# Attention, router and two expert layers on one core: gate steps spread over two head pairs, gathers and weight parts reordered at the stage change

## The chip, the cores and the metric

One NeuronCore of a Trainium2 chip runs the whole program in one launch. The metric is device time in microseconds (us), the median of several runs; lower is better. The engines are called PE (TensorE, the matrix engine), DVE (VectorE), ACT (ScalarE), POOL (GpSimd) and SP (SyncE, which here only issues DMAs).

## The reference

Three layers follow each other. First attention with pooled queries (4 batches, 8 heads, 1152 keys, head size 64; two neighbouring queries are averaged, so 576 queries a head). Its output, 2304 tokens by 512, goes through a top-1 mixture of 8 experts, and then through a bilinear layer.

```
q_pool = q.reshape(B, H, S // 2, 2, D).mean(axis=3)
attn = softmax(q_pool @ k^T / sqrt(D)) ; x = (attn @ v) as [2304, 512]
logits = x @ w_gate ; e = argmax(logits) ; g = softmax(logits)[e]
x = g * (relu(x @ w1[e]) @ w2[e])          # 8 experts, 512 -> 1024 -> 512
out = ((x @ w_a) * (x @ w_b)) @ w_out      # 512 -> 1536 -> 512
```

## The kernel before, in words

**Number format.** Every f32 operand is split into a high and a low f16 part, and a product is three f16 matmuls. The subtraction that makes a low part ("split_low", `p_low`) is elementwise work for DVE or POOL.

**Attention** runs 16 head pairs (`NPAIR`), each in 21 units (`NU`), in one loop over `n` whose code order is the order on every engine (`manual_schedule`). A pair does two things at once. It computes scores, exponentials and the product with V of pair p (lines 365 to 430). And it finds the row maxima of pair p+1: `a_units` (line 315) makes a [128, 2, 384] block of scores on PE in the PSUM pool `ps_a`, which has two buffers (tag "sa"), and DVE reduces it (line 335, 14 such reductions in a pair). `finish_max` (line 341) turns the maxima into a column of the operand, by way of the small tile `mm` (line 345). POOL makes the low parts `pl` (line 406), one per unit.

**The same two "sa" buffers** also serve the transposes `tp` of `turn` (line 486), the logits `lp` and the gate's counts `rp`. While `tp` waits for `turn_low`, the reductions have one buffer left.

**The gate** of a finished batch (four pairs) is a generator: `scales`, `gate` and `out_scale` (lines 526, 543, 605) `yield` between steps, and the attention loop calls `aside()` as often in unit u as the table `ASIDE` (line 935) says. It is started in unit 15 of pairs 4, 8 and 12. It finds the expert of each token, counts ranks with six small matmuls into `rp` (line 564), and builds for each of 5 token tiles a one-hot table `amat` [128, 128] (line 593). The gate of the last batch cannot lie beside attention: it runs at the end.

**The stage change.** After the last pair: `norm`, `mag_x`, `turn`, `scales`, `logits`, `gate`, then `route` (line 641), which computes the row numbers of the first three token groups (`find(0)`, index tile `idx0`) and the slot table `info`. Then `gather` (line 1100, an indirect DMA on POOL) reads 128 tokens from the DRAM buffer `xbuf` into a tile `xg`; `scale_x` and `x_t` (lines 1110, 1117) scale and transpose them. Ten `warm` matmuls (line 1272) stand on PE between `info` and the transposes. A conditional (line 1281) reloads the weights if expert 0 has no token; PE's first matmul of the first slot waits until ACT and DVE have passed it. Before it the code puts four `split_low` of weight parts 12 to 15 on DVE, and four `load_raw(0, i, 2)` on SP.

**The experts** run in slots of 64 tokens (`do_slot`, line 1291): `stage1`, `stage2`, `change` (which splits the next expert's weights, 24 parts at an expert's end) and `finish`. After slot 0 `find(1)` computes the other index rows on DVE and PE. From slot 24 on, three `conv_step` a slot prepare weights of the last layer (lines 774 to 792, mostly DVE).

**The last layer** (lines 1350 to 1440) is a loop of matmuls on 384 tokens a step.

Of the kernel before, what the change touches and what calls it, by code (L numbers as in the profile page):

```python
# [27 lines left out]
def attn_moe_kernel(  # L28
# [114 lines left out]
    nc.vector.tensor_scalar(out=out_id, in0=iota_part, scalar1=float(PAD), scalar2=None, op0=ALU.add)  # L143

# [22 lines left out]
    offs = rt.tile([128, E], F32, name="offs")  # L167
    idxo = rt.tile([128, NT // 128], U32, name="idxo")
# [171 lines left out]
    def finish_max(p, halves=(0, 1)):  # L340
# [4 lines left out]
        nc.vector.tensor_scalar(  # L345
            out=mm, in0=mm, scalar1=-1.0 / MC, scalar2=float(np.log(PX)) * 16.0 * SC * SC / MC, op0=ALU.mult, op1=ALU.add
        )
# [103 lines left out]
    def norm(p, j):  # L451
        b, h = bh(p)
        if h == 0 and j == 0:
            xe[b] = ap2.tile([128, NTB, XW], F32, tag="xe", name=f"xe{b}")
            lgp[b] = ap2.tile([128, NTB, HP, E], F32, tag="lgp", name=f"lgp{b}")
# [43 lines left out]
    def logits(p):  # L499
# [3 lines left out]
        for t in range(NTB):  # L503
# [6 lines left out]
        nc.vector.tensor_scalar(  # L510
            out=lgp[b][:, :, h // 2], in0=lp[:, 0 : NTB * E].rearrange("p (t e) -> p t e", e=E),
            scalar1=1.0 / (VC * VC), scalar2=None, op0=ALU.mult,
        )
# [29 lines left out]
    def gate(b):  # L543
        lg = ap2.tile([128, NTB, E], F32, tag="lg", name=f"lg{b}")
        nc.vector.tensor_reduce(out=lg, in_=lgp[b].rearrange("p t h e -> p t e h"), axis=AX.X, op=ALU.add)
# [25 lines left out]
        yield  # L571
# [20 lines left out]
        for i in range(NTB):  # L592
            (nc.gpsimd if b == B - 1 and i < 3 else nc.vector).tensor_scalar(
                out=amat[:, b, i], in0=iota_row2.rearrange("p a r -> p (a r)"), scalar1=row[:, i], scalar2=None, op0=ALU.is_equal
            )
            if i == 2:
                yield
# [16 lines left out]


    def find(i, ip):
        NB = B * NTB
        c0, n = ((0, NP0), (NP0, NP - NP0))[i]
        bm = rt.tile([128, NB, 2, n], F16, name=f"bm{i}")
        w = [128, NB, 2, n]  # L620
        nc.vector.tensor_tensor(
            out=bm, in0=slot.rearrange("p t (o a) -> p t o a", o=1).to_broadcast(w),
            in1=iota_slot[:, :, c0 : c0 + n].rearrange("p (o a) s -> p o a s", o=1).to_broadcast(w), op=ALU.is_equal,
# [231 lines left out]
    with tc.manual_schedule():  # L855
# [195 lines left out]
        for i in range(8, 12):  # L1051
            split_pool(0, i)
# [4 lines left out]
        while gates:  # L1057
            aside()
# [207 lines left out]
    with tc.manual_schedule():  # L1266
# [24 lines left out]
        def do_slot(s):  # L1291
# [15 lines left out]
            if s == 0:  # L1307
                find(1, ipb)
# [141 lines left out]
```

## Time and profile before

| | us |
|---|---|
| median of 3 runs | 1330.67 (1327.02 to 1331.19) |
| the profiled execution, its own time | 1324.79 |
| its span in the trace | 1323.1 |

| stage | stretch of the span, us |
|---|---|
| attention | 0 to 558 |
| last gate, routing, first gather | 558 to 589 |
| experts | 589 to 883 |
| last layer | 887 to 1323 |

| engine | busy, share of the span |
|---|---|
| PE | 1189.3 us, 90% |
| DVE | 788.9 us, 60% |
| ACT | 648.6 us, 49% |
| POOL | 524.8 us, 40% |

An engine is busy while an instruction of it is in flight, also when that instruction itself is held up. So two columns are read together below: the duration of an instruction against the same form elsewhere, and the idle time before it, in square brackets with the instruction that ended it. "Granted clock" is the TensorE clock in a stretch, 1.00 being 2.4 GHz and 0.50 being 1.2 GHz. Times are positions in the span.

### The profile page before, as it was taken

The numbers are of one execution on the slowest core, as the hardware profiler recorded it, in microseconds if no ns is written. First come the engines' busy times: TensorE is split into PE (matmuls) and PEld (weight loads), VectorE is DVE, ScalarE is ACT, GpSimd is POOL, SyncE is SP. The second block draws the span as 40 slices with busy tenths as digits, with TensorE's granted clock in tenths as the row PEclk, the third lists the DMA queues.
The fourth block names the chain that finished last, engine by engine and source line by source line (L and its number), as shares of the span: only waits on it lengthen the run. The fifth ranks groups of instructions, "written<-read, shape, count | busy, mean of one in ns | idle before, by whom it ended". The sixth has DMA issues, their size and how long they took to land. (4 is left out here: it accounts for less than half of the span.)

```text
span 1323.1 us, 41118 instructions
## 1 busy us (share of the span) xinstructions
PE 1189.3 (90%) x17154; PEld 827.8 (63%) x17154; DVE 788.9 (60%) x1548; ACT 648.6 (49%) x1324; POOL 524.8 (40%) x475
## 2 busy tenths in 40 slices
PE   7799997999899889748987997889999999999996
PEld 6466664665566556547977997875555555555553
DVE  4677777878777876756377248528668732222221
ACT  3577885888688768804266237315433311111111
POOL 3578885888688868742243321200000000000000
PEclk9899998999899989858988998999999999999998
DMA  7656685456465622634077226503212100000000
GB/s 170 112 129 163 141 178 138 112 114 150 101 109 132 138 58 51 216 98 155 23 273 274 71 62 199 177 13 112 96 65 96 48 1 1 24 24 25 25 17 32
DMA packets 170508, 136.46 MB, mean 103 GB/s; under 512 B 101072, under 2 KB 136400, under 8 KB 170256
## 3 DMA queue, kind: packets, MB, share of 16 engines
q1 hardware_dynamic: 167056, 122.74, 35.2%
q0 software_dynamic: 3200, 10.53, 2.4%
q8 instruction: 136, 2.23, 0.7%
q14 instruction: 116, 0.95, 0.2%
HBM read 94.96 MB, written 9.74 MB: 79 GB/s over the span
## 5 line engine op out<-in xcount | busy, mean ns | idle before, releaser
L406 POOL TENSOR_TENSOR pl<-pt,ph 128x512 f16<-128x512 f32 (+1 forms) x330 | 382.4, 1176 | 130.5 <-ACT ph L388 97.9
L335 DVE TENSOR_REDUCE mx<-sa 128x2 f32<-128x768 f32 x224 | 206.4, 924 | 87.9 <-PE sa L330 85.0
L386 ACT ACTIVATE pt<-sp 128x512 f32<-128x512 f32 (+1 forms) x336 | 197.3, 588 | 116.6 <-PE sp L379 111.5
L1360 PEld LDWEIGHTS <-wc 128*128 128x128 f16 x1728 | 169.5, 98 | 124.5 <-PEq L1322 4.4
L1360 PE MATMUL ab<-x2h,wc 128*128 128x384 f16 x1152 | 212.0, 327 | 4.3 <-PEq L1322 4.3
L428 PEld LDWEIGHTS <-ph 128*128 128x128 f16 (+1 forms) x2880 | 152.9, 102 | 77.1 <-issue 37.2
L388 ACT ACTIVATE ph<-sp 128x512 f16<-128x512 f32 (+1 forms) x331 | 194.6, 588 | 0.0
L1399 POOL DMA_INDIRECT out_dram<-ob,idxo x18 | 17.7, 982 | 442.2 <-DVE ob L1398 409.8
L330 PE MATMUL sa<-kst,qq 128*128 128x384 f16 x480 | 162.2, 338 | 29.2 <-DVE mx L335 25.8
L428 PE MATMUL av<-vv,ph 128*128 128x65 f16 (+2 forms) x2880 | 170.3, 197 | 0.0
L330 PE MATMUL sa<-kst,qlt 128*128 128x384 f16 x480 | 161.4, 337 | 0.0
L428 PE MATMUL av<-vv,pl 128*128 128x65 f16 (+1 forms) x1440 | 157.9, 196 | 1.3 <-POOL pl L406 1.3
L1370 DVE TENSOR_TENSOR gf<-ab,sa 128x384 f32<-128x384 f32 x72 | 40.1, 557 | 192.5 <-PE ab L1360 192.5
L379 PE MATMUL sp<-rl,k2b 66*128 66x512 f16 (+1 forms) x576 | 138.9, 295 | 9.4 <-DMA rl<-qln 8.8
L376 PE MATMUL sp<-qq,kst 128*128 128x512 f16 (+1 forms) x576 | 138.2, 294 | 8.3 <-ACT ph L388 8.2
L1161 PEld LDWEIGHTS <-w2c 128*128 128x128 f16 x3840 | 127.2, 101 | 25.5 <-issue 18.3
L1140 PE MATMUL hp<-xh,w1c 128*128 128x64 f16 x2560 | 126.9, 195 | 8.1 <-DVEq L1281 2.5
L1140 PEld LDWEIGHTS <-w1c 128*128 128x128 f16 x3840 | 122.2, 100 | 14.0 <-DVE w1c L847 5.4
L428 PEld LDWEIGHTS <-pl 128*128 128x128 f16 (+1 forms) x1440 | 124.9, 103 | 1.6 <-POOL pl L406 1.6
L1140 PE MATMUL hp<-xl,w1c 128*128 128x64 f16 x1280 | 123.4, 195 | 1.6 <-issue 1.6
L1360 PE MATMUL ab<-x2l,wc 128*128 128x384 f16 x576 | 117.5, 327 | 0.0
L1161 PE MATMUL yp<-hh,w2c 128*128 128x64 f16 x2560 | 111.3, 198 | 5.6 <-ACT hh L1146 4.7
(229 smaller groups left out, 1813.5 us busy)
## 6 DMA issues: line engine op xcount, KB each, us to landing
raw<-in_moe_w_dram SPq DMA_DIRECT2D x20, 1024.0 KB, 6.5
rbw<-in_moe_w_dram SPq DMA_DIRECT2D x20, 1024.0 KB, 6.9
kr<-in_k_dram SPq DMA_DIRECT2D x16, 576.0 KB, 5.1
vr<-in_v_dram SPq DMA_DIRECT2D x16, 576.0 KB, 5.8
qr<-in_q_dram SPq DMA_DIRECT2D x32, 256.0 KB, 3.4
cl<-in_moe_w_a_dram SPq DMA_DIRECT2D x12, 512.0 KB, 3.5
cl<-in_moe_w_b_dram SPq DMA_DIRECT2D x12, 512.0 KB, 3.5
cl<-in_moe_w_out_dram SPq DMA_DIRECT2D x12, 512.0 KB, 3.6
```

Of the source, the lines that this page charges most:

```text
L330: nc.tensor.matmul(sa[:, i, :KA], lhsT=x[:, 128 * b_ : 128 * b_ + 128], rhs=kst[:, j, ks], start=o == 0, stop=o == len(ops) - 1,)
L335: nc.vector.tensor_reduce(out=s["mx"].rearrange("p t n -> p (t n)")[:, ones[0] : ones[0] + m].rearrange("p (m o) -> p m o", o=1), in_=sa[: ...
L376: nc.tensor.matmul(sp[:, o : o + w], lhsT=s["kst"][:, j, ks], rhs=s["qq"][:, c0 : c0 + w], start=True, stop=False)
L379: nc.tensor.matmul(sp[:, o : o + w], lhsT=k2b[p % 3][:, j, ks], rhs=s["rl", j if w > 64 else 1][0:66, c0 : c0 + w], start=False, stop=True,)
L386: nc.scalar.activation(pt[:, :o], sp[:, :o], AF.Exp, scale=1.0 / (16.0 * SC * SC))
L388: nc.scalar.activation(phb[n % NPB][0][:, :o], sp[:, :o], AF.Exp, scale=1.0 / (16.0 * SC * SC))
L406: eng.tensor_tensor(out=l[:, :w], in0=pts.pop(n)[:, :w], in1=h[:, :w], op=ALU.subtract)
L428: nc.tensor.matmul(o, lhsT=a, rhs=b_, start=first, stop=False, skip_group_check=True)
L1140: nc.tensor.matmul(hp[:, j], lhsT=wc[:, t, i], rhs=g[x][:, i, w], start=first, stop=(j == 3 and i == KD - 1 and x == "xl"), skip_group_che ...
L1161: nc.tensor.matmul(y[:, d], lhsT=wc[:, t, 128 * d : 128 * d + 128], rhs=hs[s, n][x][:, j], start=first, stop=(n == 1 and len(terms) == 1 a ...
L1360: nc.tensor.matmul(ps[:, 0:TB], lhsT=w_[:, t, m, 128 * i : 128 * i + 128], rhs=x_[:, i, ts_], start=(i + j == 0), stop=(j == 2 and i == KD ...
L1370: nc.vector.tensor_tensor(out=gf, in0=pair[1], in1=sa, op=ALU.mult)
```

## The change

The parts, in the order of the program:

- `mm` and the one-hot tables `amat` on DVE: an instruction with two tensor inputs in place of one with one tensor input.
- `lgp` sums the four logits products as they come, and the later reduction (`lg`) falls away.
- The gate's steps get more `yield`s, and `ASIDE` one call in every second unit; each of the five `amat` has a step of its own. `norm_tail` moves from unit 5 to 6.
- Two of the four parts that POOL split at the end of attention go to DVE.
- `xgb`, the gathers' targets, move from the pool `mp`, which shares memory with attention's tiles, to `rt`, which doesn't. The first `scale_x` goes to ACT.
- The conditional stands ahead of the four `split_low` and the four `load_raw`.
- `find(1)` is cut in two: its DVE part after slot 0, its matmuls after slot 1.
- `conv_step`s start at slot 17.

```
+    lpx = cst.tile([128, 9, 1], F32, name="lpx")          # memset to the added constant
+    xgb = [rt.tile([128, XW], F32, name=f"xg{i}") for i in range(3)]     # was mp.tile
 finish_max:
-        nc.vector.tensor_scalar(out=mm, in0=mm, scalar1=-1.0 / MC, scalar2=..., op0=ALU.mult, op1=ALU.add)
+        nc.vector.scalar_tensor_tensor(out=mm, in0=mm, scalar=-1.0 / MC, in1=lpx, op0=ALU.mult, op1=ALU.add)
 logits:
+        if h == 0:
+            nc.vector.tensor_scalar(out=lgp[b], in0=l_, scalar1=1.0 / (VC * VC), scalar2=None, op0=ALU.mult)
+        else:
+            nc.vector.scalar_tensor_tensor(out=lgp[b], in0=l_, scalar=1.0 / (VC * VC), in1=lgp[b], op0=ALU.mult, op1=ALU.add)
 gate:
-        lg = ap2.tile([128, NTB, E], F32, tag="lg", name=f"lg{b}")
-        nc.vector.tensor_reduce(out=lg, in_=lgp[b].rearrange("p t h e -> p t e h"), axis=AX.X, op=ALU.add)
+        lg = lgp[b]
...
         nc.vector.tensor_reduce(out=fm, in_=o, axis=AX.X, op=ALU.max)
+        yield
         nc.vector.tensor_tensor(out=o, in0=desc_, in1=fm.to_broadcast([128, NTB, E]), op=ALU.is_equal)
+        yield
+
+        yield
         yield
...
-        yield                                              # between the rp matmuls and the ranks
...
         for i in range(NTB):
-            (nc.gpsimd if b == B - 1 and i < 3 else nc.vector).tensor_scalar(
-                out=amat[:, b, i], in0=iota_row2..., scalar1=row[:, i], scalar2=None, op0=ALU.is_equal
-            )
-            if i == 2:
-                yield
+            if b == B - 1 and i < 3:
+                nc.gpsimd.tensor_scalar(out=amat[:, b, i], in0=io, scalar1=row[:, i], scalar2=None, op0=ALU.is_equal)
+            else:
+                nc.vector.tensor_tensor(out=amat[:, b, i], in0=io, in1=row[:, i].to_broadcast([128, 128]), op=ALU.is_equal)
+            yield
 attention loop:
-        ASIDE = [1, 0, 1, 0, 0, 1, 0, 1, 0, 0, 1, 0, 1, 0, 0, 1, 1, 0, 1, 1, 2]
+        ASIDE = [1, 0] * (NU // 2) + [1]
-            n0=13, n1=4, nt=5, ...
+            n0=13, n1=4, nt=6, ...
 end of attention:
-        for i in range(8, 12):
+        for i in range(10, 12):
             split_pool(0, i)
...
+        split_low(0, 8)
         turn_low(NPAIR - 1)
+        split_low(0, 9)
         logits(NPAIR - 1)
 scale_x:
-        (nc.gpsimd if pr else nc.vector).tensor_scalar(out=g["xs"]..., scalar1=g["x"][:, DM : DM + 1], ...)
+        if pr:
+            nc.gpsimd.tensor_scalar(...)
+        else:
+            nc.scalar.activation(xs_, g["x"][:, 0:DM], AF.Copy, scale=g["x"][:, DM : DM + 1])
 before slot 0:
         x_t(0)
-        for i in range(12, 16):
-            split_low(0, i)
-        for i in range(4):
-            load_raw(0, i, 2)
         e0 = field("n0", 0, wengs, E - 1)
         with tc.If(e0 > 0):
...
+        for i in range(12, 16):
+            split_low(0, i)
+        for i in range(4):
+            load_raw(0, i, 2)
 do_slot:
             if s == 0:
-                find(1, ipb)
+                find(1, ipb, (0,))                         # the two DVE instructions that make bm
+            if s == 1:
+                find(1, ipb, (1,))                         # 20 matmuls and the index conversion
             if 2 <= s < NU64 - 1:
...
-                for _ in range(3 if s >= 24 else 0):
+                for _ in range(3 if s >= 17 else 0):
```

Three places show the moves. Rows of before carry line numbers of the kernel before; rows of the change carry its own, which are 3 to 24 higher.

DVE in the pair after a gate has started, before (`mx` the maxima, `sa_14` and `sa_16` the score blocks, `xtl` the end of `norm_tail`):

```order
L475 RECIPROCAL rec<-rec 64x1
L477 TENSOR_SCALAR xtl<-av_9_3277,rec 64x64
L593 TENSOR_SCALAR amat<-iota_row_106,row_3603 128x128 x3
L335 TENSOR_REDUCE mx_3379<-sa_14_3738 128x2
L593 TENSOR_SCALAR amat<-iota_row_106,row_3603 128x128 x2
L598 TENSOR_TENSOR val<-tok_base,row_3603 128x5
L335 TENSOR_REDUCE mx_3379<-sa_16_3774 128x2
```

DVE at the same place with the change (`rp` the counts, `rank` the ranks), and then a later stretch in the pair after that:

```order
L478 TENSOR_SCALAR xtl<-av_9_3282,rec 64x64
L338 TENSOR_REDUCE mx_3380<-sa_14_3720 128x2
L338 TENSOR_REDUCE mx_3380<-sa_16_3753 128x2
L580 TENSOR_REDUCE tot_3773<-rp_3765 128x8
L581 TENSOR_TENSOR rank_3772<-rp_3765,run 128x40
```

```order
L603 TENSOR_TENSOR amat<-iota_row_106,row_3890 128x128
L338 TENSOR_REDUCE mx_4035<-sa_0_4036 128x2
L603 TENSOR_TENSOR amat<-iota_row_106,row_3890 128x128
L338 TENSOR_REDUCE mx_4035<-sa_2_4101 128x2
L258 SCALAR_TENSOR_TENSOR vv_215<-vr_3553,vv_215 128x9x64
L338 TENSOR_REDUCE mx_4035<-sa_4_4137 128x2
L603 TENSOR_TENSOR amat<-iota_row_106,row_3890 128x128 x2
L338 TENSOR_REDUCE mx_4035<-sa_6_4185 128x2
```

The three `amat` in a row ahead of `sa_14` are gone from there; `tot` and `rank`, which stood behind `sa_4` of the same run of blocks, come behind `sa_16`, and the five `amat` are spread over the stretch in which the next pair begins.

DVE between attention and the first slot, before (`osc` the last attention result, `xl` the low part of the first tokens, `w2c` the weight parts; the last two rows are the conditional):

```order
L612 SCALAR_TENSOR_TENSOR osc<-gs_10594 128x5
L1112 TENSOR_SCALAR xs_10630<-xg_10627 128x512
L1124 SCALAR_TENSOR_TENSOR xl_10633<-xt_10646,xh_10632 128x512
L847 SCALAR_TENSOR_TENSOR w2c_9831<-raw_154,w2c_9831 128x512
L847 SCALAR_TENSOR_TENSOR w2c_9832<-raw_154,w2c_9832 128x512
L847 SCALAR_TENSOR_TENSOR w2c_9833<-raw_154,w2c_9833 128x512
L847 SCALAR_TENSOR_TENSOR w2c_9834<-raw_154,w2c_9834 128x512
L1168 TENSOR_LOAD info
L1281 COMPARE_AND_BRANCH
```

The same place with the change:

```order
L620 TENSOR_TENSOR gs_10589<-gs_10589,am_10441 128x5
L621 SCALAR_TENSOR_TENSOR osc<-gs_10589 128x5
L1145 SCALAR_TENSOR_TENSOR xl_10625<-xt_10638,xh_10624 128x512
L1189 TENSOR_LOAD info
L1298 COMPARE_AND_BRANCH
```

`xs` has gone to ACT, and the four `w2c` come after the conditional.

DVE after slot 0, before (`x2l` the slot's result, `bm`, `idf`, `idx` the rest of the indices, `hl` of the next slot):

```order
L1178 SCALAR_TENSOR_TENSOR x2l<-yp_10650,x2h 128x4x64
L621 TENSOR_TENSOR bm_11198<-slot,iota_slot 128x760
L625 TENSOR_TENSOR bm_11198<-bm_11198,val 128x760
L636 TENSOR_SCALAR idf_11221<-ipb,pad_id 64x19 x2
L639 CAST idx_142<-idf_11221 128x19
L1147 SCALAR_TENSOR_TENSOR hl_0_10641<-hp_10648,hh_0_10640 128x256
```

With the change:

```order
L1199 SCALAR_TENSOR_TENSOR x2l<-yp_10642,x2h 128x4x64
L652 TENSOR_TENSOR bm_11190<-slot,iota_slot 128x760
L656 TENSOR_TENSOR bm_11190<-bm_11190,val 128x760
L1168 SCALAR_TENSOR_TENSOR hl_0_10633<-hp_10640,hh_0_10632 128x256
L1168 SCALAR_TENSOR_TENSOR hl_1_10635<-hp_10641,hh_1_10634 128x256
```

`idf` and `idx` follow one slot later, and with them the 20 matmuls on PE from which they come.

## Rows read from the trace of the kernel before

**Rows 1.** Head pairs: stretch, length; busy PE, PEld, DVE, ACT, POOL; clock, DMA, GB/s

```profile
294.26:323.58 29.32, 28.30 (x428) 18.93 (x425) 23.29 (x41) 24.84 (x52) 26.09 (x25) 1.00 0.65 156
193.98:234.84 40.86, 32.36 (x435) 20.94 (x432) 33.60 (x71) 25.33 (x53) 25.20 (x23) 0.87 0.49 123
...
453.92:494.20 40.28, 32.37 (x434) 20.90 (x431) 32.97 (x70) 25.33 (x53) 25.21 (x23) 0.87 0.31 68
```

**Rows 2.** PE timeline, plain pair, then gate pair: start, us, instruction, [idle before]

```profile
181.59 0.32 PE L330 MATMUL sa<-kst,qq 128*128 128x384 f16 x1 [0.81 <-DVE mx L335]
...
199.14 0.32 PE L330 MATMUL sa<-kst,qq 128*128 128x384 f16 x1 [1.31 <-DVE mx L335]
...
202.96 0.19 PE L564 MATMUL rp<-oh,ones 128*128 128x40 f16 x1 [2.58 <-DVE oh L558]
...
219.72 0.48 PE L330 MATMUL sa<-kst,qq 128*128 128x384 f16 x1 [4.00 <-DVE mx L335]
```

**Rows 3.** DVE timeline around the first gate

```profile
164.00 1.00 DVE L345 TENSOR_SCALAR mm<-mm 128x9 f32<-128x9 f32 x1
...
199.01 0.42 DVE L545 TENSOR_REDUCE lg<-lgp 128x40 f32<-128x160 f32 x1
...
201.80 1.10 DVE L558 TENSOR_TENSOR oh<-desc,gfm 128x40 f16<-128x40 f32 x1
...
215.51 3.16 DVE L593 TENSOR_SCALAR amat<-iota_row,row 128x128 f16<-128x128 f32 x3
...
219.58 0.47 DVE L593 TENSOR_SCALAR amat<-iota_row,row 128x128 f16<-128x128 f32 x2
```

**Rows 4.** POOL timeline of the same stretch

```profile
163.82 1.16 POOL L406 TENSOR_TENSOR pl<-pt,ph 128x512 f16<-128x512 f32 x1 [0.25 <-ACT ph L388]
...
201.70 1.15 POOL L406 TENSOR_TENSOR pl<-pt,ph 128x512 f16<-128x512 f32 x1 [2.22 <-issue]
...
214.10 4.49 POOL L406 TENSOR_TENSOR pl<-pt,ph 128x512 f16<-128x512 f32 x4
```

**Rows 5.** PE timeline from the end of attention to the second slot

```profile
542.30 0.47 PE L489 MATMUL tp<-ident,xe 128*128 128x128 f32 x1 [1.88 <-DMA xe<-xtl]
...
577.45 4.61 PE L1272 MATMUL yp<-ones_sq 128*128 128x128 f32 x20 [0.73 <-DVE gs L607]
583.74 1.09 PE L1121 MATMUL xt<-ident,xs 128*128 128x128 f32 x4 [1.69 <-issue]
...
588.83 0.23 PE L1140 MATMUL hp<-xh,w1c 128*128 128x64 f16 x1 [2.51 <-DVEq L1281]
...
599.27 0.66 PE L629 MATMUL ipb<-bm,amat 128*128 128x38 f16 x20 [2.77 <-DVE bm L625]
```

**Rows 6.** The other engines' timelines of that stretch, by start

```profile
572.44 0.17 DVE L639 CAST idx<-idf 128x3 uint32<-128x3 f32 x1
...
578.07 0.17 DVE L612 SCALAR_TENSOR_TENSOR osc<-gs 128x5 f32<-128x5 f32 x1
...
579.28 1.20 POOL L1102 DMA_INDIRECT xg<-xbuf,idx  x1 [8.81 <-issue]
...
583.15 0.49 DVE L1112 TENSOR_SCALAR xs<-xg 128x512 f32<-128x512 f32 x1 [4.92 <-DMA xg<-xbuf,idx]
...
585.62 0.69 DVE L1124 SCALAR_TENSOR_TENSOR xl<-xt,xh 128x512 f16<-128x512 f32 x1 [1.98 <-ACT xh L1123]
586.23 2.49 DVE L847 SCALAR_TENSOR_TENSOR w2c<-raw,w2c 128x512 f16<-128x512 f32 x4
```

**Rows 7.** Stages after the wait at 599.27, columns as in rows 1

```profile
600.00:602.00 2.00, 2.00 (x43) 2.00 (x40) 0.62 (x3) 0.00 (x0) 1.01 (x1) 0.50 0.00 0
602.00:604.00 2.00, 2.00 (x52) 2.00 (x50) 0.42 (x1) 0.38 (x1) 0.00 (x0) 0.66 0.52 140
```

**Rows 8.** Stages, three slots with two expert changes: without and with conversions

```profile
690.10:718.11 28.01, 22.55 (x592) 21.37 (x592) 24.53 (x43) 20.93 (x43) 8.11 (x5) 0.88 0.85 302
800.73:833.43 32.70, 23.36 (x590) 22.18 (x587) 30.51 (x56) 23.64 (x49) 6.50 (x4) 0.84 0.78 267
```

More of the change, by code (lines that the diff above doesn't have):

```diff
@@ L454, in norm @@
             xe[b] = ap2.tile([128, NTB, XW], F32, tag="xe", name=f"xe{b}")
-            lgp[b] = ap2.tile([128, NTB, HP, E], F32, tag="lgp", name=f"lgp{b}")
+            lgp[b] = ap2.tile([128, NTB, E], F32, tag="lgp", name=f"lgp{b}")
             nc.gpsimd.memset(xe[b][64:128, 4], 0.0)
@@ L509, in logits @@
                 )
[L510 to L513, printed above, removed]
+        l_ = lp[:, 0 : NTB * E].rearrange("p (t e) -> p t e", e=E)
+        if h == 0:
+            nc.vector.tensor_scalar(out=lgp[b], in0=l_, scalar1=1.0 / (VC * VC), scalar2=None, op0=ALU.mult)
+        else:
+            nc.vector.scalar_tensor_tensor(
+                out=lgp[b], in0=l_, scalar=1.0 / (VC * VC), in1=lgp[b], op0=ALU.mult, op1=ALU.add
+            )
     def store_x(b, h0, h1):
@@ L592, in gate @@
         for i in range(NTB):
[L593 to L597 removed]
+            io = iota_row2.rearrange("p a r -> p (a r)")
+            if b == B - 1 and i < 3:
+                nc.gpsimd.tensor_scalar(out=amat[:, b, i], in0=io, scalar1=row[:, i], scalar2=None, op0=ALU.is_equal)
+            else:
+                nc.vector.tensor_tensor(
+                    out=amat[:, b, i], in0=io, in1=row[:, i].to_broadcast([128, 128]), op=ALU.is_equal
+                )
+            yield
         nc.vector.tensor_tensor(
@@ L613, in out_scale, with find @@
         yield
-    def find(i, ip):
+    bms = {}
+    def find(i, ip, halves=(0, 1)):
         NB = B * NTB
         c0, n = ((0, NP0), (NP0, NP - NP0))[i]
-        bm = rt.tile([128, NB, 2, n], F16, name=f"bm{i}")
+        if 0 in halves:
+            bms[i] = rt.tile([128, NB, 2, n], F16, name=f"bm{i}")
+        bm = bms[i]
         w = [128, NB, 2, n]
-        nc.vector.tensor_tensor(
-            out=bm, in0=slot.rearrange("p t (o a) -> p t o a", o=1).to_broadcast(w),
-            in1=iota_slot[:, :, c0 : c0 + n].rearrange("p (o a) s -> p o a s", o=1).to_broadcast(w), op=ALU.is_equal,
-        )
-        nc.vector.tensor_tensor(
-            out=bm, in0=bm, in1=val.rearrange("p b i (o a) -> p (b i) o a", o=1).to_broadcast(w), op=ALU.mult
-        )
+        if 0 in halves:
+            find_places(bm, w, c0, n)
+        if 1 not in halves:
+            return
         for t in range(NB):
@@ L639, in find, with find_places @@
         nc.vector.tensor_copy(idxs[i], idf)
+    def find_places(bm, w, c0, n):
+        nc.vector.tensor_tensor(
+            out=bm, in0=slot.rearrange("p t (o a) -> p t o a", o=1).to_broadcast(w),
+            in1=iota_slot[:, :, c0 : c0 + n].rearrange("p (o a) s -> p o a s", o=1).to_broadcast(w), op=ALU.is_equal,
+        )
+        nc.vector.tensor_tensor(
+            out=bm, in0=bm, in1=val.rearrange("p b i (o a) -> p (b i) o a", o=1).to_broadcast(w), op=ALU.mult
+        )
     def route():
@@ L1085, in attn_moe_kernel @@
     mps = mo_ctx.enter_context(tc.tile_pool(name="mps", bufs=1, space=PSUM))
-    xgb = [mp.tile([128, XW], F32, name=f"xg{i}") for i in range(3)]
     xsb = [mp.tile([128, KD, 128], F32, name=f"xs{i}") for i in range(2)]
```

11 lines of the change are left out of this document (4 added, 7 removed).

## The prediction

> **What bounds the kernel now.** I read the table of stages first, then the timelines of PE and DVE in the stages that stand out, and then the other engines at the places where PE waits.
>
> The stages [rows 1] cut attention at the same instruction of each head pair. A plain pair takes 29.32 us; PE is busy for 28.30 of them at a granted clock of 1.00, so PE sets it, and DVE has 6.0 us idle. Three pairs hold a gate; the first takes 40.86 and the last 40.28, 11.5 and 11.0 more, and with the one between, which is as long as the first, that is 34.1 in all. In the first, PE is busy for 4.1 more (32.36) because the clock is 0.87, and idle for 7.5 more. DVE has 10.3 us more work (33.60). So a gate pair is lost by stalls that DVE causes, and by the clock that comes down after them.
>
> PE's timeline [rows 2] shows where. In the plain pair the block behind the transposes waits 0.81 for a maximum. In the gate pair there are waits of 1.31 (a maximum), 2.58 (`rp` waits for the one-hot `oh`) and 4.00 (a maximum behind the three `amat`). The last stands where `tp` holds one of the two "sa" buffers: the block `sa_16` can't start until `sa_14` has been reduced, so a microsecond of DVE work ahead of that reduction is a microsecond on PE.
>
> DVE's rows [rows 3] are long for what they do: 1.00 for `mm`, a tiny tile, and 1.10 for `oh`, an instruction with two tensor inputs; 3.16 for three `amat`, but 0.47 for two. POOL explains it [rows 4]: the `mm` at 164.00 ends at 165.00 and POOL's `pl` at 164.98; the `oh` at 201.80 ends at 202.90 and POOL's at 202.85; the three `amat` lie inside 4.49 us of `pl`. While POOL works on such a tile, DVE instructions with one f32 input from SBUF and those with two both wait for its end.
>
> After attention PE's timeline [rows 5] has the seam. The last result of attention (`osc`) is done at 578.24, the index tile already at 572.61 [rows 6], yet the gather starts at 579.28: its target shares memory with attention's tiles. The transposes `xt` come at 583.74, `xl` at 585.62, then four `w2c` up to 588.72, then the conditional, and slot 0 starts at 588.83. At 599.27 PE waits 2.77 for `bm`, and then the clock is 0.50 for two microseconds and 0.66 for two more [rows 7]. Among the experts, three slots with two expert changes take 28.01 without and 32.70 with conversions, DVE busy going from 24.53 to 30.51 [rows 8].
>
> **Gates.** Two-input instructions in place of one-input ones: both wait for POOL [rows 3, 4], so I take 0 for `mm` and `amat` themselves. The summed `lgp` removes the reduction `lg`, 0.42 a gate [rows 3].
>
> By the Trainium skill, "VectorE: DVE Perf Modes", section "The perf-mode tier table (the rule you actually need)", a f32 tensor_scalar passes two elements a cycle and a tensor_tensor one. As an estimate from that page, 128 columns at 0.96 GHz are 67 ns more for each of 15 `amat`, 1 us of DVE in all; no run here shows it yet.
>
> The spread is what counts. The 10.3 us of DVE work go over two pairs, 5.1 each, less than the 6.0 that DVE has idle in a plain pair, so the sum fits; but it delays PE wherever a step stands directly ahead of a reduction without slack. There are two such places a pair: at `sa_14`, and between `sa_16` and `sa_18`, where `rp` now takes its buffer and `tot` and `rank` follow. In the first pair I take one held-up instruction of 1.1 [rows 3] at each: 2.2. In the second pair the end of `scales` (`gs`, again 1.1) and about two `amat` at 0.85 more than their free 0.24 each: 2.8. For the clock a quarter of the 4.1: stalls of 1 us left it at 1.00 in the plain pair, a longer one may still happen. That is 6.0 a gate instead of 11.4, 18 in all: a gain of 34.1 − 18 = **16**. Bounds: if everything but one held-up instruction in each pair and 0.8 of chance fits into DVE's idle time, 3 a gate, gain 25; if every stall is moved and none shrinks, 11.4 a gate, gain 0.
>
> **End of attention.** `norm_tail` moves a unit later, behind a `pl`. In the last pair PE waits 1.88 for its transfer [rows 5], so this wait grows: −**0.5** (0 to −2). In other pairs the place is behind `sa_14` anyway.
>
> **Seam.** The gather no longer waits for attention's memory: it can start at about 573 instead of 579.28 and its rows land 3.87 later (583.15 − 579.28), at about 577. This is now early, and `xs` on ACT with it; what is late next is the row of warm matmuls, 577.45 to 582.06 [rows 5]. `xt` follows at 582.06, `xl` 1.88 later, 0.69 long [rows 6], and with the `w2c` behind the conditional slot 0 starts 0.11 after: 584.7, a gain of 4.1. Ahead of it, DVE gets two splits of 0.62 (a quarter of the 2.49 of four), half of which stand in time that DVE waits; it loses `lg`, and fewer splits on POOL hold up about half an instruction less: net gain 0.4. The four `w2c` and the raw loads behind the conditional are wanted late in the first expert's weights; slot 0's first matmuls cover their 2.49. If they don't, that much comes back.
>
> The cut of `find(1)` lets DVE make `bm` under slot 0 and 1: the 2.77 go, and with them the low clock, 2 × 0.50 + 2 × 0.34 = 1.7 [rows 7]. Its matmuls and conversions come a slot later and are wanted by the second gather only. Seam: 4.5 + 2.8 + 1.7 = **9** (5, if the `w2c` stall slot 0 and part of the clock stays; 12, if the warm matmuls end earlier too).
>
> **Experts.** The 30 conversions now go to slots 17 to 26, which hold no expert change; the 32.70 go back towards 28.01, 4.7, and I leave 0.7 for ten slots with more DVE work: **4** (2 to 5).
>
> **The sum.** 16 − 0.5 + 9 + 4 = 28.5. The profiled execution's own time is 1324.79, so 1296.3; the median of the runs shown is 1330.67, 0.44% above it, so in those terms **1302.0**. The last layer isn't touched.
>
> **The rivals.**
>
> *Two-input instructions don't wait for POOL.* For it: the new forms, a broadcast column and a constant column, don't stand in the trace. Against it: the 1.10, which ends with POOL's tile to 0.05 us [rows 3, 4]. It would bring `mm` from 1.00 to 0.2 in each of 15 pairs, mostly hidden, and the gates to about 2.5 each: 10.5 more, about **1291**. Chance 0.07. The Trainium skill, "Perfetto Trace Analysis", section "Optimizing Scalar/DVE Operations", reads this way: it gives the lock to 2-port operations, which a two-tensor one is not. By that page the change removes the waits; the two rows (`oh` and the `pl` beside it) speak against it.
>
> *The spread is worth nothing.* Both pairs keep a stall of several microseconds, the clock comes down in both, and a gate still costs 11.4. For it: the "sa" buffers stay as short, and `rp` takes one in a worse place. Then 1330.67 − 12.5 = **1318**. Chance 0.08.
>
> *Slower.* Each of the two pairs becomes as long as the one gate pair is now: a step at `sa_14`, one at `rp`, a stall over 2.5 in each and a clock of 0.87 in both. A gate then costs 22.8, 34.1 more in all, less 12.5 from the seam and the experts: about **1352**. It decides from 11.4 + 12.5 / 3 = 15.6 a gate on. Against it: only 5.1 us of DVE work come into a pair. Chance 0.03.
>
> *The seam is not relieved*: the gather stays held by another wait, or the change has its memory shared again. Then the seam gives 4.5 instead of 9, with the other terms: **1306**. Inside the range; chance 0.05. No change at all, 0.02, would need both this and the spread failing.
>
> **How the numbers follow.** The forecast has 0.75, with a range of its own from the gates (±8), the seam (±3), the experts and the last pair (±2) taken as independent: 1293 to 1311. The range, 1287 to 1313, takes in the first rival and the seam's, and leaves out the second and the third and the far ends of the gates. About 0.3%, 4 us, is what a measurement of this kernel can tell from no change. Faster 0.95: forecast, the first two rivals and the seam's; same 0.02; slower 0.03.
>
> **What would show it.** In the stages of the changed kernel: two pairs of about 32 us for each gate in place of one of 41, both at a clock above 0.95; `amat` and `mm` still at about 1 us when POOL is busy (at 0.2 the first rival is right); no wait of 4 us at `sa_16`. The gather starting by 574; slot 0 by 585; no wait of 2.8 for `bm`. Three slots with two changes back at 28. A gate pair with a wait over 2.5 and a clock of 0.87, or a slot 0 after 587, would make the prediction wrong.

## The result and the profile after

The changed kernel takes 1307.9 us (median of 4 runs, 1304.91 to 1310.28), the kernel before in the same comparison 1328.85: a ratio of 0.985, 95% interval 0.981 to 0.989. The forecast was 1302.0, 0.978 of the 1330.67 that it started from. The profiled spans are 1323.1 and 1304.1 us, so 19.0 us are there to be placed. The two traces are cut at the same instructions, and the table lays the stretches side by side. The "result" of a slot is its first instruction on `x2h`.

| stretch | before | after | gain | forecast |
|---|---|---|---|---|
| start of the program to the second `mm` | 51.22 | 48.90 | 2.3 | 0 |
| the pair that begins at 99.66 before, the first in which PE waits long for `norm_tail` | 35.04 | 32.33 | 2.7 | 0 |
| three gates, two pairs each | 210.24 | 199.04 | 11.2 | 16 |
| the other attention pairs | | | −0.8 | 0 |
| last `mm` to the result of slot 0 | 74.25 | 68.51 | 5.7 | 4.0 |
| results of slot 0 to slot 2 (`find(1)`) | 21.89 | 20.20 | 1.7 | 4.5 |
| slot 2 to slot 16 | 107.29 | 108.01 | −0.7 | 0 |
| slot 16 to slot 31 (conversions) | 107.71 | 108.46 | −0.8 | 4 |
| slot 31 to the end | 489.7 | 492.1 | −2.4 | 0 |

The gate pairs of the changed kernel, in the table of stages (length; busy PE, PEld, DVE, ACT, POOL; clock, DMA, GB/s), a pair of rows for the first and the last gate:

```profile
189.87:224.36 34.49, 31.26 (x444) 20.64 (x441) 31.30 (x59) 25.91 (x55) 26.95 (x23) 0.95 0.56 146
224.36:257.30 32.94, 29.11 (x415) 19.22 (x413) 26.65 (x51) 24.06 (x50) 24.86 (x23) 0.95 0.51 110
...
442.05:476.74 34.69, 31.40 (x444) 20.64 (x441) 31.36 (x60) 25.91 (x55) 26.95 (x23) 0.95 0.37 79
476.74:506.81 30.07, 27.27 (x415) 18.46 (x413) 23.02 (x47) 22.29 (x45) 23.19 (x21) 1.00 0.16 42
```

Against [rows 1] one pair of 40.9 and a plain one have become two of 33 to 34.5 in the first gate, and the clock is 0.95 instead of 0.87. The 40.86 + 29.31 of the first gate are now 34.49 + 32.94. But there is still a long wait, which PE's timeline shows, and which answers to the 4.00 in [rows 2]:

```profile
208.28 0.32 PE L333 MATMUL sa<-kst,qq 128*128 128x384 f16 x1 [1.23 <-DVE mx L338]
210.14 0.19 PE L571 MATMUL rp<-oh,ones 128*128 128x40 f16 x1 [0.62 <-DVE mx L338]
...
243.60 0.32 PE L333 MATMUL sa<-kst,qq 128*128 128x384 f16 x1 [3.55 <-DVE mx L338]
```

DVE's timeline ahead of that matmul, in the second pair of the gate:

```profile
240.49 0.96 DVE L620 TENSOR_TENSOR gs<-gs,am 128x5 f32<-128x5 f32 x1
241.48 1.07 DVE L621 SCALAR_TENSOR_TENSOR osc<-gs 128x5 f32<-128x5 f32 x1
242.58 0.96 DVE L338 TENSOR_REDUCE mx<-sa 128x2 f32<-128x768 f32 x1
```

And POOL's:

```profile
238.04 4.49 POOL L407 TENSOR_TENSOR pl<-pt,ph 128x512 f16<-128x512 f32 x4
```

The gate's last step stands directly ahead of the reduction of `sa_14`, and its two instructions of five columns take 2.0 us because POOL is at work until 242.53. The place and the mechanism are those of [rows 3, 4]; only the instructions are others. All three gates have this wait (3.55, 3.56, 2.73); in the third only one of the two instructions is held up, and the clock stays at 1.00.

The seam, PE's timeline:

```profile
560.88 4.44 PE L1293 MATMUL yp<-ones_sq 128*128 128x128 f32 x20 [0.73 <-DVE gs L616]
...
567.86 0.20 PE L1161 MATMUL hp<-xh,w1c 128*128 128x64 f16 x1 [1.00 <-DVEq L1298]
...
590.32 0.21 PE L1182 MATMUL yp<-hl,w2c 128*128 128x64 f16 x1 [2.31 <-DVE hl L1168]
```

and POOL's:

```profile
555.95 1.20 POOL L1122 DMA_INDIRECT xg<-xbuf,idx  x1 [2.90 <-DVE v L680]
```

The gather starts 0.3 us after its indices (555.65), where it had waited 6.7 [rows 6]. From the first warm matmul to the matmul behind the conditional, from which slot 0 runs on without a break, it is 7.0 us instead of 11.4 [rows 5]. The 2.77 at `bm` is gone; instead PE waits 2.31 for `hl` one slot later, and the clock falls there too (0.50 in the table of stages for the next four microseconds):

```profile
590.00:592.00 2.00, 1.68 (x33) 1.68 (x33) 2.00 (x5) 0.08 (x1) 1.01 (x1) 0.50 1.04 382
592.00:594.00 2.00, 2.00 (x42) 2.00 (x40) 1.00 (x2) 0.00 (x0) 0.00 (x0) 0.50 1.07 400
```

The conversions, in the table of stages of the kernel before (slots 16 to 28) and of the changed kernel (the same, then the three slots of [rows 8]):

```profile
725.72:800.73 75.01, 73.06 (x2355) 72.51 (x2355) 25.96 (x59) 20.08 (x47) 20.54 (x20) 1.00 0.21 63
```

```profile
703.53:783.97 80.44, 74.52 (x2355) 73.06 (x2355) 39.87 (x85) 25.05 (x56) 22.61 (x20) 1.00 0.29 91
783.97:811.99 28.02, 23.07 (x590) 21.46 (x587) 23.91 (x43) 21.04 (x44) 8.37 (x4) 0.88 0.71 251
```

The three slots came back from 32.70 to 28.02 as forecast, but the twelve slots ahead of them went from 75.01 to 80.44, with 13.9 us more work on DVE.

### The profile page after: what moved, and what is told of

It reads as the page before. It is cut to its first block, busy times and chain, and to the rows that moved or that the text cites. A ratio compares the mean times of both kernels' runs of the same rounds, so it can differ in the third digit from the quotient of the medians.

```text
span 1304.1 us, 41111 instructions
## 1 busy us (share of the span) xinstructions
PE 1181.3 (91%) x17154; PEld 823.2 (63%) x17154; DVE 798.9 (61%) x1546; ACT 648.2 (50%) x1325; POOL 525.3 (40%) x471
## 5 line engine op out<-in xcount | busy, mean ns | idle before, releaser
L333 PE MATMUL sa<-kst,qq 128*128 128x384 f16 x480 | 159.1, 332 | 29.1 <-DVE mx L338 25.3
L333 PE MATMUL sa<-kst,qlt 128*128 128x384 f16 x480 | 158.7, 331 | 0.0
L1182 PE MATMUL yp<-hh,w2c 128*128 128x64 f16 x2560 | 114.0, 199 | 8.3 <-issue 3.6
```

What stands on the lines that cost most here:

```text
L333: nc.tensor.matmul(sa[:, i, :KA], lhsT=x[:, 128 * b_ : 128 * b_ + 128], rhs=kst[:, j, ks], start=o == 0, stop=o == len(ops) - 1,)
L1182: nc.tensor.matmul(y[:, d], lhsT=wc[:, t, 128 * d : 128 * d + 128], rhs=hs[s, n][x][:, j], start=first, stop=(n == 1 and len(terms) == 1 a ...
```

## The experiments

The runs come from two chips: the changed kernel again, the run with `lg` and the shared pool, the one with the weight parts and the one with fewer warm matmuls ran on the second, the others on the first. So times are compared as ratios to the kernel before on the same chip, whose medians there were 1322.3 and 1328.2, and the causes are read from the stages of the profiles. The changed kernel was run again as one of them:

> The changed kernel itself, unaltered, beside the other runs of this call: 0.985 of the kernel before within 0.003. Its profile shows what differs between two executions of one kernel: the stretches before the first gate and the expert slots are expected within 1 us of the first profile, the clock after a wait of about 2 us may fall or not.

It gave 1306.55 us, 0.985 (0.981 to 0.989). Its gate pairs sum to 199.3 (199.0 in the first profile), and from the result of slot 16 to that of slot 31 it takes 106.2 (108.5), from slot 2 to slot 16 110.1 (108.0): the expert slots differ by 2 us between two executions, more than I expected. Seven profiles with the changed kernel's gate give sums of 198.1 to 202.7: that is the scatter against which the following are read.

**The last step of the gate.**

```
 out_scale:
         nc.vector.tensor_scalar(out=gs, in0=gs, scalar1=1e-9, ...)
         yield
+        yield
+        yield
+        yield
         nc.vector.reciprocal(gs, gs)
```

> The gate's last step (three small DVE instructions that end in osc) comes three calls later, so that it no longer stands ahead of the reduction of sa_14 in the second pair of each gate. Theory: that step, held up by POOL, makes the waits of 3.55, 3.56 and 2.73 us on PE and with the first two the clock of 0.95. Then the second pairs go from 32.94, 34.01 and 30.07 to about 29.6, 31.0 and 28.3, and the kernel gains 7 to 9 us against the changed kernel. Rival: the wait comes from the two buffers, whatever stands on DVE; then it stays over 2 us in some place of the second pair and less than 3 us are gained.

1298.21 us, 0.9815 (0.980 to 0.983). PE's timeline and the stages of the first gate:

```profile
241.32 0.32 PE L333 MATMUL sa<-kst,qq 128*128 128x384 f16 x1 [1.23 <-DVE mx L338]
```

```profile
190.52:224.43 33.91, 30.02 (x444) 19.72 (x441) 31.88 (x60) 26.04 (x55) 26.95 (x23) 1.00 0.58 149
224.43:254.39 29.96, 27.84 (x414) 18.35 (x413) 25.75 (x51) 23.96 (x50) 25.12 (x23) 1.00 0.55 121
```

The wait went from 3.55 to 1.23 and the clock is 1.00 in all six pairs. The second pairs take 29.96, 31.67 and 29.77, the six sum to 193.2. So the step's place cost about 6 us by the stages, a little under what was expected. By the ratios it is 4 to 5 us, and there the intervals of this run and of the changed kernel overlap; the stages decide, and the two later runs with the step moved have sums of 191.0 and 192.5. No wait over 2 us is left in the second pairs, so the rival is out.

**The gate packed as before.** The old table and the old yields, in the changed kernel:

```
-        ASIDE = [1, 0] * (NU // 2) + [1]
+        ASIDE = [1, 0, 1, 0, 0, 1, 0, 1, 0, 0, 1, 0, 1, 0, 0, 1, 1, 0, 1, 1, 2]
```

> The gate's steps are cut and called as in the kernel before (the old table and the old yields), with the two-input instructions kept. Forecast of the prediction: the spread is worth 16 us. Theory now: three gates go back to one pair of 40 to 41 us and a plain second pair, slower by 10 to 12 us, and the stretch before the first gate does not change. Rival: the two-input instructions are what shortened the gates; then the packed gate pairs stay under 38 us.

1304.3 us, 0.988 (0.986 to 0.990). My theory fell: the gate pairs are 38.95, 37.70 and 36.87, not 40 to 41, and with their second pairs they sum to 201.6, inside the scatter of the changed kernel's. With `lg` gone, spreading the steps gains hardly anything. Its DVE timeline has the one-hot `oh` unhindered, where [rows 3] have 1.10, and PE's waits at `rp` and `sa_16` are 1.31 and 4.32, where [rows 2] have 2.58 and 4.00:

```profile
196.76 0.20 DVE L561 TENSOR_TENSOR oh<-desc,gfm 128x40 f16<-128x40 f32 x1
```

```profile
197.02 0.21 PE L567 MATMUL rp<-oh,ones 128*128 128x40 f16 x1 [1.31 <-DVE oh L561]
...
213.86 0.48 PE L333 MATMUL sa<-kst,qq 128*128 128x384 f16 x1 [4.32 <-DVE mx L338]
```

**Packed, and with `lg`.** The packed run, with the reduction and the separate logits parts that it sums put back:

```
+        lg = ap2.tile([128, NTB, E], F32, tag="lg", ...)
+        nc.vector.tensor_reduce(out=lg, in_=lgp[b].rearrange("p t h e -> p t e h"), axis=AX.X, op=ALU.add)
-        lg = lgp[b]
```

> The run with the gate's steps packed, with the reduction lg and the separate logits parts put back as well; the two-input instructions stay. Theory: the 0.42 us of lg is what the packed gate pairs (38.95, 37.70, 36.87) had gained on the 40.9 of the kernel before: with it the one-hot oh comes half a microsecond later, meets POOL's tile, and PE's wait at rp goes from 1.3 back to 2.6. Then the pairs are 40 to 41 again and the kernel loses 5 to 9 us against the packed run without lg. Rival: the two-input instructions or the later norm_tail shortened the pairs; then they stay below 39 and the loss is under 2 us.

1312.99 us, 0.993 (0.991 to 0.995), 0.5% slower than the packed run. DVE's and POOL's timelines of the second gate, and PE's:

```profile
324.87 0.42 DVE L546 TENSOR_REDUCE lg<-lgp 128x40 f32<-128x160 f32 x1
...
327.66 1.10 DVE L559 TENSOR_TENSOR oh<-desc,gfm 128x40 f16<-128x40 f32 x1
```

```profile
327.55 1.15 POOL L407 TENSOR_TENSOR pl<-pt,ph 128x512 f16<-128x512 f32 x1 [2.22 <-issue]
```

```profile
328.82 0.19 PE L565 MATMUL rp<-oh,ones 128*128 128x40 f16 x1 [2.58 <-DVE oh L559]
```

and the stage of the first gate:

```profile
189.81:230.43 40.62, 31.81 (x434) 20.63 (x431) 34.26 (x70) 25.33 (x53) 25.35 (x23) 0.92 0.51 124
```

With `lg`, `oh` starts 0.1 us after a POOL tile and waits for its end; without it, it is over before the next tile starts (196.96; POOL's tile and PE's `rp` both start at 197.02). As long as the steps are packed, a reduction of 0.42 us decides over 2 to 3 us a gate: the six pairs go from 201.6 to 209.5, and 210.24 was the kernel before. So the larger part of what the prediction put down to the spread can be had without it.

One run is missing for the rest: the spread with `lg` left in. In the spread order `oh` is a step of its own and takes 0.28 in all three gates, and it was not tried whether `lg` would change that. The spread may therefore gain these 8 us by itself too, in another way; how the 11.2 divide between the two parts is open.

**One input again.** `mm` and `amat` as `tensor_scalar`:

```
-        nc.vector.scalar_tensor_tensor(out=mm, in0=mm, scalar=-1.0 / MC, in1=lpx, op0=ALU.mult, op1=ALU.add)
+        nc.vector.tensor_scalar(out=mm, in0=mm, scalar1=-1.0 / MC, scalar2=..., op0=ALU.mult, op1=ALU.add)
```

> mm and the one-hot tables are one-input instructions again; all else as in the changed kernel. Forecast of the prediction: no difference, since both forms wait for POOL (mm has a median of 0.94 us in the changed kernel, 1.00 before); the time stays within 2 us, and the mm median stays at 0.9 to 1.0. Rival of the prediction (two-input instructions don't wait): slower by about 10 us and mm at 1.0 against 0.2. By the estimate from the page on perf modes: faster by up to 1 us.

1303.22 us, 0.985 (0.981 to 0.989), the ratio of the changed kernel. The instructions of `mm` (minimum, median and longest in ns), in the changed kernel and in this run:

```profile
L348 DVE SCALAR_TENSOR_TENSOR mm<-mm,lpx x17: 170/944/1011, 24.4 to 506.8; 128x9 f32<-128x9 f32 x17
```

```profile
L348 DVE TENSOR_SCALAR mm<-mm x17: 172/949/1020, 24.4 to 511.8; 128x9 f32<-128x9 f32 x17
```

For `mm` both forms are held alike, as forecast. For the tables `amat` they are not:

```profile
L603 DVE TENSOR_TENSOR amat<-iota_row,row x17: 275/284/1247, 221.5 to 551.2; 128x128 f16<-128x128 f32 x17
```

```profile
L605 DVE TENSOR_SCALAR amat<-iota_row,row x17: 270/962/1253, 222.6 to 556.3; 128x128 f16<-128x128 f32 x17
```

The medians are 0.28 and 0.96. The second table of the first gate shows where they part, DVE and POOL in the changed kernel, then in this run:

```profile
224.90 0.29 DVE L603 TENSOR_TENSOR amat<-iota_row,row 128x128 f16<-128x128 f32 x1
224.91 4.48 POOL L407 TENSOR_TENSOR pl<-pt,ph 128x512 f16<-128x512 f32 x4 [0.38 <-PE sp L380]
```

```profile
225.93 1.25 DVE L605 TENSOR_SCALAR amat<-iota_row,row 128x128 f16<-128x128 f32 x1
225.95 2.91 POOL L409 TENSOR_TENSOR pl<-pt,ph 128x512 f16<-128x512 f32 x3 [0.39 <-PE sp L382]
```

DVE's instruction starts 0.01 to 0.02 us ahead of POOL's tile in both; the two-input form passes, the one-input form is held to the tile's end, in all three gates. Where POOL's tile has begun before it, the two-input form is held too: 1.25 for the first table of each gate in the changed kernel, 1.23 to 1.27 for the first three in the packed run. So in the changed order the two-input tables take 2.5 us of DVE a gate, the one-input ones 3.9 to 5.4. That cost no time that can be told: the gate pairs sum to 202.7, the highest of the seven profiles but only 1 us above the next, and the ratio is the same. The prediction's estimate from the Trainium skill, "VectorE: DVE Perf Modes", section "The perf-mode tier table (the rule you actually need)", 67 ns more for a table with two inputs, doesn't show: where POOL holds neither, two in a row start 0.19 us apart with one input and 0.20 with two.

**Find whole.**

```
-                find(1, ipb, (0,))
-            if s == 1:
-                find(1, ipb, (1,))
+                find(1, ipb)
```

> find(1) stands whole after slot 0 again; all else as in the changed kernel. Forecast of the prediction: PE waits 2.8 us for bm again and the clock falls after it, slower by 4.5 us. Theory now: the changed kernel has a wait of 2.3 us for hl and a clock of 0.50 for some microseconds one slot later, so slots 1 and 2 together lose only 1 to 2 us by it.

1308.14 us, 0.990 (0.988 to 0.992). From the result of slot 0 to that of slot 2 it takes 22.85 us against 20.20 and 20.27 in the changed kernel: the cut is worth 2.6. PE waits 2.90 for `bm` again; the wait for `hl` is 1.55 here, and 2.31 with the cut. By the ratios the whole time rose by about 7 us, with intervals that just touch; the profiled span did not (1304.0, the fastest of the four executions), so the rest isn't explained by this run.

**Conversions from slot 24.**

```
-                for _ in range(3 if s >= 17 else 0):
+                for _ in range(3 if s >= 24 else 0):
```

> The conversions start at slot 24 again; all else as in the changed kernel. Forecast of the prediction: slower by 4 us. Theory now: the conversions only moved their cost. Slots 17 to 26 get 5 to 6 us back, the three slots from the end of slot 28 go from 28.0 to 32.7 us, and the time is that of the changed kernel within 2 us.

1302.51 us, 0.985 (0.983 to 0.987), the changed kernel's ratio. The stages, slots 16 to 28 and the three after:

```profile
701.62:776.81 75.19, 72.93 (x2355) 72.47 (x2355) 26.04 (x59) 20.07 (x47) 20.54 (x20) 1.00 0.21 62
776.81:810.82 34.01, 24.49 (x588) 23.15 (x585) 30.49 (x56) 23.64 (x48) 6.25 (x4) 0.81 0.76 268
```

Together 109.2, against 108.5 and 106.2 in the two profiles of the changed kernel. The early start took 6 us off the three slots and put 3.3 to 5.3 on the twelve ahead of them; it saved at most 3.

**Conversions ahead of the slot's end**, and the gate's last step later as in the first run:

```
+            if 2 <= s < NU64 - 1:
+                for _ in range(3 if s >= 17 else 0):
+                    conv_step(c_left)
             finish(s)
...
-                for _ in range(3 if s >= 17 else 0):
-                    conv_step(c_left)
```

> The gate's last step three calls later, as in the first run, and the three conversion steps of a slot put ahead of the slot's end instead of behind it, so that on DVE they stand in the idle time before x2l and not ahead of the next hl. Theory: the 12 slots from slot 16 to 28 go from 77.5 to between 75 and 76, the expert changes after them stay at 28 to 29, and the kernel gains 2 us against the first run. Rival: DVE is short of time in these slots wherever the steps stand; then they stay at 77 or more and nothing is gained.

1290.71 us, 0.978 (0.974 to 0.983), 7.5 us under the first run on the same chip, whose interval it overlaps.

```profile
694.42:768.15 73.73, 72.81 (x2355) 72.38 (x2355) 39.34 (x85) 26.43 (x56) 22.60 (x20) 1.00 0.33 100
768.15:796.84 28.69, 22.40 (x590) 20.28 (x587) 24.58 (x43) 21.05 (x44) 6.34 (x4) 0.94 0.72 245
```

The same DVE work (39.34 us) costs nothing in the twelve slots when it stands ahead of `x2l`: 73.73 for PE's 72.81, and 75.17 in the next run that has this order (fewer warm matmuls, below), where ten profiles with the steps behind the slot's end have 77.4 to 80.4. So DVE isn't short of time there; the place was wrong. Of the 9 us between the profiled spans of this run and of the first, 4.6 lie from slot 16 to slot 31; 2.2 are in the gate pairs, which is in the scatter.

**Gather targets in the shared pool.**

```
-    xgb = [rt.tile([128, XW], F32, name=f"xg{i}") for i in range(3)]
+    xgb = [mp.tile([128, XW], F32, name=f"xg{i}") for i in range(3)]
```

> The gather targets lie in the pool that shares memory with attention's tiles again; all else as in the changed kernel. Forecast of the prediction: the first gather starts after osc again, some 7 us after the indices, xt comes 2 us after the last warm matmul, and slot 0 starts 3 to 4 us later. Rival: the 5 us that the stage change gained come from the conditional's new place; then slot 0 starts less than 1 us later.

1303.17 us, 0.986 (0.984 to 0.989). The forecast failed: the gather starts 0.3 us after its indices (557.14) all the same, and slot 0 starts 7.3 us after the warm matmuls' start instead of 7.0. That is the rival's number, but not for its reason, since the gather was never held up here:

```profile
557.44 1.20 POOL L1122 DMA_INDIRECT xg<-xbuf,idx  x1 [2.89 <-DVE v L679]
```

**The shared pool with the old neighbours.** The packed run with `lg`, with the gather targets in the shared pool, and `norm_tail` set back a unit (`nt=6` to `nt=5`):

> The packed run with lg, and in addition the gather targets back in the shared pool and norm_tail back in unit 5. The gather targets alone, put back, did not make the gather wait; theory: what it waited for in the kernel before depends on the neighbours in memory, and with lg and the four-part lgp back, the targets lie over the gate's last tiles again. Then the gather starts over 6 us after its indices, behind osc, and slot 0 starts 2 us or more later against the warm matmuls. Rival: the wait came from something else (the first scaling on DVE, say); then the gather starts 0.5 us after its indices. On norm_tail: if unit 5 made the pair at 99 us of the kernel before long (35.0, in all later runs 32 to 34), it is 35 again here, otherwise 32 to 33.

1321.04 us, 0.995 (0.993 to 0.997). Now the gather waits: indices at 569.5, `osc` done at 575.1, gather at 576.19, 1.1 us behind `osc` as in the kernel before [rows 6]. POOL's timeline, and PE's:

```profile
576.19 1.20 POOL L1118 DMA_INDIRECT xg<-xbuf,idx  x1 [9.29 <-SPq L1294]
```

```profile
574.34 3.94 PE L1289 MATMUL yp<-ones_sq 128*128 128x128 f32 x20 [0.73 <-DVE gs L611]
...
583.88 0.24 PE L1157 MATMUL hp<-xh,w1c 128*128 128x64 f16 x1 [0.95 <-DVEq L1294]
```

Slot 0 starts 9.5 us after the warm matmuls' start, against 7.1 in the packed run with `lg`: the gather is worth 2.4. So the move of the targets removes the wait (the packed run with `lg` has it gone, this one has it back), and so does something else in the change, since the targets alone, put back, did not bring it back. That this is the smaller tiles of the logits, by which the targets come to lie over other tiles, is inferred; the gate's old table and `norm_tail` in unit 5 also set this run apart from the one with the targets alone, and no row names the tile. And the pair with the first stall of `norm_tail` is long again. In the kernel before, and in this run (PE's timeline, then the stage):

```profile
123.96 0.33 PE L489 MATMUL tp<-ident,xe 128*128 128x128 f32 x1 [1.89 <-DVE axl L497]
```

```profile
122.40 0.33 PE L489 MATMUL tp<-ident,xe 128*128 128x128 f32 x1 [1.88 <-DVE axl L497]
```

```profile
98.11:133.18 35.07, 32.21 (x461) 21.19 (x459) 27.78 (x47) 27.38 (x56) 28.77 (x25) 0.95 0.66 151
```

With `norm_tail` in unit 6 the wait is 1.54 and the pair 32.33 at a clock of 1.00 in the changed kernel, and the same within 0.02 in ten of the eleven other profiles with unit 6. The eleventh is the run with the gather targets in the shared pool and nothing else put back; the changed kernel and that run (PE's timeline, then the stage):

```profile
121.02 0.33 PE L490 MATMUL tp<-ident,xe 128*128 128x128 f32 x1 [1.54 <-DVE axl L498]
```

```profile
97.82:130.15 32.33, 30.41 (x460) 20.42 (x458) 27.35 (x46) 27.04 (x56) 28.57 (x25) 1.00 0.64 153
```

```profile
121.69 0.33 PE L489 MATMUL tp<-ident,xe 128*128 128x128 f32 x1 [1.53 <-DVE axl L497]
```

```profile
98.51:132.44 33.93, 32.02 (x460) 21.28 (x458) 27.33 (x46) 27.37 (x56) 29.22 (x25) 0.95 0.63 146
```

So of the 2.7 us 0.9 are idle time of PE and 1.8 busy time at the lower clock, and the clock can fall at the shorter wait too. Both profiles with unit 5 have the shared pool as well; `norm_tail` alone was not put back, so that the unit is worth all of the 2.7 is likely but not shown. In the last pair PE waits 2.76 where [rows 5] have 1.88; but that wait, for a DMA, is anywhere from 0.74 to 3.19 in the profiles with unit 6 and 0.69 in the second one with unit 5, so a cost of the move doesn't show there.

**Weight parts ahead of the conditional.** The four `split_low` and the four `load_raw` back ahead of it:

> The four w2c splits on DVE and the four raw loads stand ahead of the conditional again; all else as in the changed kernel. Theory: these 2.5 us of DVE and what SP issues stand between xl and PE's first matmul of slot 0, so slot 0 starts 2 to 3 us later after the warm matmuls than in the changed kernel (567.9, 7.0 after their start at 560.9). Rival: PE's start hangs on the warm matmuls alone; then it moves by less than 0.7 us.

1305.73 us, 0.983 (0.979 to 0.986). Slot 0 starts 9.0 us after the warm matmuls' start, 2.0 later than in the changed kernel:

```profile
569.48 0.24 PE L1161 MATMUL hp<-xh,w1c 128*128 128x64 f16 x1 [2.60 <-DVEq L1302]
```

But the result of slot 2 comes 35.2 us after the start of the warm matmuls, against 34.6 and 34.5: slot 1 takes 10.2 instead of 11.8 and gives it back. This part of the change moved 2 us and kept half a microsecond.

**Fewer warm matmuls**, in the run with the conversions ahead of the slot's end:

```
-        for _ in range(10):
+        for _ in range(4):
```

> The best run so far (last gate step later, conversions ahead of the slot's end) with 4 warm matmuls instead of 10. With the gather early, the transposes xt stand behind the 4.3 us of warm matmuls and for nothing else: with four of them xt comes 2.5 us earlier and slot 0 too. Theory: 2 us faster than the run with 10. Rival: without them the clock stays low through slot 0 and gives the 2 us back.

1293.79 us, 0.974 (0.970 to 0.978); the changed kernel took 1306.55 on the same chip. PE's timeline:

```profile
557.43 2.04 PE L1296 MATMUL yp<-ones_sq 128*128 128x128 f32 x8 [0.74 <-DVE gs L616]
...
562.44 0.24 PE L1164 MATMUL hp<-xh,w1c 128*128 128x64 f16 x1 [0.97 <-DVEq L1301]
```

Slot 0 starts 5.0 us after their start instead of 6.6, and the result of slot 9 comes 74.4 after it instead of 76.4. So with the early gather it was the warm matmuls that were late. The rival is right in part: from the warm matmuls' start to slot 0 the granted clock is 0.50 instead of 0.75, and slot 0 itself takes 8.0 instead of 7.5. But then the wait for `hl`, 2.31 in the run with ten, is 0.36. The intervals of this run and of the one with ten overlap, so the 2 us are shown by the stages and not by the times. This is the lowest ratio of all runs: about 1.0% under the changed kernel and 2.6% under the kernel before.

## Why the prediction came out as it did

The sign and the range were right, and the point was 6 us too low: 0.985 lies between the forecast's 0.978 and the range's upper end (1313 of 1330.67, 0.987). The terms were less right than their sum.

- **What bounds the kernel**: right. DVE steps ahead of what PE waits for, held up by POOL, and the clock after it set the gate pairs; taking `lg` and the gate's last step out of the way shortened them by 8 and by 6 us.
- **Two-input forms at 0**: right in time, and for `mm` in mechanism (0.94 us in the changed kernel, 0.95 with one input). For `amat` the reading was too simple: in the spread order the two-input tables have a median of 0.28 and the one-input ones 0.96, so the sign "still at about 1 us" held for the first table of a gate only. The first rival is out, since two-input instructions are held too where POOL's tile has begun before them. The Trainium skill, "Perfetto Trace Analysis", section "Optimizing Scalar/DVE Operations", names only a 2-port operation as holding the lock; the 0.96 and 1.07 of instructions with two inputs beside POOL's tiles show that these wait as well. The Trainium skill, "SBUF — State Buffer", section "SBUF: two separate sides", counts operations with two SBUF inputs among those that contend, against GpSimd operations that read SBUF; the same two numbers agree with that.
- **Gates, 16**: measured 11.2. The term that was mis-sized is "`lg`, 0.42 a gate", taken as a length. With the steps packed, its 0.42 decide whether `oh` meets a POOL tile, and are worth 8 us over three gates (209.5 against 201.6). With `lg` gone, the spread, which I gave the 16, is worth between nothing and 3; what it would be worth with `lg` was not run.
- **The second pair, 2.8 a gate**: the place was named (`gs` held up, at `sa_14`), the size was not. Two held-up instructions in a row give a wait of 3.55 and a clock of 0.95. A gate cost 7.6 more than plain pairs (199.04 less 176.1, by three) where I had 6.0; with the step elsewhere it is 5.7. I had counted instructions, and should have counted which of them stand at the place without slack. Of my signs of being wrong, "a wait over 2.5 and a clock of 0.87", the wait came and the clock didn't.
- **`norm_tail`, −0.5**: lost in the scatter of the last pair. But the pair at 99.66 gained 2.7, which I had not looked at: it is 5.7 longer than a plain pair, and my list of stages left it out.
- **Seam, the start of slot 0, 4.5**: measured 4.4 from the warm matmuls on. The gather's part is 2.4, since the warm matmuls cover the rest, and the order at the conditional has 2.0. That the second would come back was in the lower bound, and most of it did, in slot 1.
- **`find(1)`, 4.5**: measured 1.7 against the kernel before, 2.6 against the cut undone. The wait at `bm` went, but one slot later PE waits for `hl`, 2.31 instead of 1.54, and the clock falls there. I had named nothing that is late next.
- **Experts, 4**: measured −0.8 in the first profile and 1.5 in the second. The term "0.7 for ten slots with more DVE work" was 2.4 to 5.4 over ten profiles: I took DVE's idle share in those slots for room, but the conversions stand ahead of `hl`, on which PE waits.
- **Not in the prediction**: 2.3 us less at the start, and 2.4 more at the end. Later runs, one of them with `lg`, the old table and `norm_tail` in unit 5, end the first stretch anywhere from 48.5 to 50.3, so I put it down to differences between executions; the kernel before has one profile only. At the end, PE waits 2.10 before the first matmul on `o` of the last layer where it had waited 1.72, and the clock is 0.56 to 0.59 in the four microseconds after it instead of 1.00. Two of the later runs waited 2.09 there and stayed at 1.00; why the wait is 1.72 or 2.1 isn't shown.

So the gates, `find(1)` and the conversions fell 12 us short of their terms. Against that stood 1.7 more than forecast at the stage change and an unforeseen 2.7 in one pair; the differences at the start and at the end cancel. The range was wide enough for that; the point was not better founded.

## What to carry to other kernels

Price a step by what stands directly behind it on its engine and how much slack that has, not by its length or by the engine's idle share: a reduction of 0.42 us was worth 8 us, and 14 us of conversions were free or cost 2 to 5 depending on the side of one instruction on which they stood. Where a small step may be held up by another engine, move it behind the instruction that a third engine waits for, and look at every stage that is longer than its plain neighbour, also the one that is not on the list. When a wait is removed, name what is late next; here it was filler matmuls put in for the clock. And where two parts of a change may remove the same wait, run each without the other before giving either the gain.

## What the runs showed of the hardware

A POOL tile of 1.15 us holds up a DVE instruction that starts 0.1 us after it for nearly its whole length (1.10 for 40 columns), while the same instruction, when it comes a quarter of a microsecond ahead of such a tile, takes 0.20. Where the two start within 0.02 us of each other, a table of 128 columns took 0.28 to 0.29 with two inputs and 1.25 with one, in all three gates. And the clock does not follow the length of a wait alone: at the same wait of PE for `axl` (the low part that DVE makes in `turn_low`), 1.53 to 1.54 us, the pair ran at 1.00 (32.3 us) in the changed kernel and at 0.95 (33.9 us) in the run with the shared gather targets. So 1.6 us between two profiles can hang on the clock without a longer wait.
